# The first feed-forward layers of a sigmoid-attention and gated feed-forward kernel: plain products over 512 tokens against one level of Strassen's algorithm over pairs of batches

## The chip, the cores and the metric

The kernel runs on one core of one Trainium2 chip. A core has a matrix engine (TensorE, PE in the profile, with its weight loads apart as PEld), three engines for element-wise work (VectorE or DVE, ScalarE or ACT, GpSimd or POOL), a queue engine (SyncE or SP) that issues nearly all DMAs here, and 16 DMA engines between DRAM and the on-chip memory SBUF. TensorE writes to PSUM, which DVE and ACT can read and POOL can't. The metric is the device time of one execution in microseconds (us), lower is better.

## The reference

Two stages follow each other: attention with a sigmoid in place of the softmax, and a gated feed-forward layer.

```
def _attn_ref(q, k, v):                       # q, k, v: (8, 12, 448, 64)
    S = q.shape[2]
    scores = q @ k.transpose(0, 1, 3, 2) / sqrt(64) - log(S)
    attn = 1 / (1 + exp(-scores))
    return attn @ v

def _moe_ref(x, w_gate, w_val, w_out):        # x: (3584, 768); w: (768, 1536), (768, 1536), (1536, 768)
    gate = 1 / (1 + exp(-(x @ w_gate)))
    val = x @ w_val
    return gate * val @ w_out
```

x is the attention's output, 8 batches of 448 tokens, with the 12 heads of 64 side by side as 768 columns. The weights come as 64-bit floats, the rest as 32-bit floats. In the kernel each operand of the feed-forward layers is split into a part `hi`, rounded to the type fp32r, and a rest `lo`, and a product is three matmuls: lo x hi, hi x lo, hi x hi.

## The kernel before

Everything is kept transposed: a tile has 128 features as its partitions and tokens along its row. The order on each engine is that in which the code is written (`manual_schedule`); engines meet at semaphores only. One queue, SP, carries the loads and stores in order, and a DMA at its head that has to wait holds up those behind it.

**Attention.** 24 pairs of two heads' pairs (m), each in 7 beats (g). A beat is four score products (L218), one sigmoid over 128x896 on ACT (L221), and the value products of two beats earlier (L235). At the end of a head pair ACT copies one PSUM tile (L245), DVE adds the other (L252), and the result goes to DRAM as x (`store_x`, L189). Beside this run the steps of a generator that turns 64-bit weight words into `hi` and `lo`: a chunk of 128x384 takes eight DVE instructions (L99 to L102, L112 to L114, L118) and one cast on POOL (L141). In this stage it converts the weights of the first 7 of 12 blocks j of 128 hidden features (`convert_tiles`), and they stay in SBUF.

**Feed-forward.** Tokens are taken 512 at a time, 7 tiles t. Part one goes over the 7 tiles with the first 7 blocks, part two with the last 5 (`late`), whose weights are converted during part one, stored to DRAM and fetched back at its end. For each block, `ff_in` computes gate and value (18 matmuls each, L321), then the sigmoid on ACT (L324), the product on DVE (L325), and the split into hh on ACT and hl on DVE (L328, L329). `ff_out` then sums over the blocks for each of 6 output tiles (L339). Part one stores these sums as `part` (L344, L345), part two loads them back and adds them (L362). At the change of a token tile x is split again: xh on ACT (L180), xl on DVE (L181). PSUM has four buffers (`mm`) for all of it.

## Time and profile before

| | |
|---|---|
| median of 3 runs | 1293.74 us (1293.4 to 1294.04) |
| the profiled execution | 1293.55 us, of which the span of its instructions is 1291.5 us |
| granted TensorE clock over the span | 1.0 |
| TensorE matmuls | 7240, busy 1285.3 us |
| DVE, ACT, POOL busy | 464.5, 358.7, 37.5 us |
| DMA | 152.14 MB, mean 118 GB/s |

In the rows of the profile `out<-in 128x512 f32 xN | busy, mean ns | idle` stands for N instructions of one line and shape, their summed time, the mean of one, and the time for which their engine stood idle just before them, with what ended it. Matmuls overlap in the pipeline, so the distance from one start to the next, and not the mean duration, is what a matmul costs. In a timeline the first two numbers are start and duration in us.

### The profile page before, as it was taken

The page shows a single profiled execution, that of the slowest core. Times are in us where ns is not written, and L with a number is a line of the kernel's source. Part 1 is how long each engine was busy: PE and PEld are TensorE (multiplying, and loading weights), DVE is VectorE, ACT ScalarE, POOL GpSimd, SP SyncE. Part 2 cuts the span into 40 slices and gives each one's busy share as a digit, 9 for nine tenths or more (in the row PEclk, how much of TensorE's full clock was granted, in tenths as well). Part 3 has the DMA queues.
Part 4 walks back from the last instruction along what each step waited for, and adds up shares of the span by engine and source line. Part 5 has one row for each costly group of instructions (what it writes and reads, how often), then busy time and mean ns, then how long its engine had stood idle before and what let it go on. Part 6 is the DMA issues. An engine that isn't in the chain of part 4 may idle for free.

```text
span 1291.5 us, 17704 instructions
## 1 busy us (share of the span) xinstructions
PE 1285.3 (100%) x7240; PEld 1003.8 (78%) x7240; DVE 464.5 (36%) x921; ACT 358.7 (28%) x505; POOL 37.5 (3%) x52
## 2 busy tenths in 40 slices
PE   9999999999999999999999999999999999999998
PEld 4445666688888888888888888888888888888887
DVE  6778777345154252461310111202231313131311
ACT  6777777712112112121121121212020201111110
POOL 1112111000000000000000000000000000000000
PEclk9999999999999999999999999999999999999999
DMA  8788777343332332422002015241404131222202
GB/s 299 244 261 279 244 235 234 132 146 96 111 98 86 116 94 77 142 95 102 25 25 74 1 46 201 104 174 54 147 8 139 33 114 49 98 66 82 74 25 81
DMA packets 70928, 152.14 MB, mean 118 GB/s; under 512 B 9408, under 2 KB 26688, under 8 KB 70848
## 3 DMA queue, kind: packets, MB, share of 16 engines
q1 hardware_dynamic: 70704, 150.90, 34.8%
q8 instruction: 56, 0.92, 0.3%
q14 instruction: 24, 0.20, 0.0%
q10 hardware_dynamic: 144, 0.13, 0.0%
HBM read 106.17 MB, written 44.83 MB: 117 GB/s over the span
## 4 chain that ended last, share of the span: by engine, by line
PE 99%; ACT 0%; DVE 0%; DVEq 0%; issue 0%
PE acc L321 53%; PE acc L339 27%; PE av L235 10%; PE sc L218 10%; PE sc L272 0%; ACT a L221 0%; DVE zeros L67 0%; DVE ob L362 0%; DVEq L423 0%; DVE bias L65 0%
## 5 line engine op out<-in xcount | busy, mean ns | idle before, releaser
L321 PE MATMUL acc<-xh,gv 128*128 128x512 f32 x2016 | 623.0, 389 | 0.0
L321 PEld LDWEIGHTS acc<-xh,gv 128*128 128x128 f32 x2016 | 378.5, 188 | 79.2 <-issue 0.7
L321 PE MATMUL acc<-xl,gv 128*128 128x512 f32 x1008 | 392.1, 389 | 0.0
L339 PE MATMUL acc<-hh,wo 128*128 128x512 f32 x1008 | 312.6, 389 | 0.0
L325 DVE TENSOR_TENSOR g<-acc,g 128x512 f32<-128x512 f32 x84 | 58.1, 692 | 598.4 <-PE acc L321 598.4
L339 PEld LDWEIGHTS acc<-hh,wo 128*128 128x128 f32 x1008 | 189.3, 188 | 39.3
L321 PEld LDWEIGHTS acc<-xl,gv 128*128 128x128 f32 x1008 | 189.3, 188 | 39.1
L218 PE MATMUL sc<-qk 64*64 64x448 f32 x1344 | 204.5, 537 | 0.4 <-ACT a L221 0.4
L235 PE MATMUL av<-a,v 64*64 64x448 f32 x1344 | 204.5, 536 | 0.0
L339 PE MATMUL acc<-hl,wo 128*128 128x512 f32 x504 | 196.1, 389 | 0.0
L221 ACT ACTIVATE a<-sc,bias 128x896 f32<-128x896 f32 x168 | 169.3, 1009 | 66.3 <-PE sc L218 62.9
L328 ACT CAST hh<-g 128x512 fp32r<-128x512 f32 x84 | 52.1, 621 | 355.2 <-DVE g L325 355.2
L324 ACT ACTIVATE g<-acc 128x512 f32<-128x512 f32 x84 | 50.3, 599 | 338.2 <-PE acc L321 338.2
L218 PEld LDWEIGHTS sc<-qk 64*64 64x64 f32 x1344 | 80.0, 133 | 52.1 <-issue 24.0
L235 PEld LDWEIGHTS av<-a,v 64*64 64x64 f32 x1344 | 80.5, 133 | 51.2 <-issue 28.1
L339 PEld LDWEIGHTS acc<-hl,wo 128*128 128x128 f32 x504 | 94.6, 188 | 19.6
L329 DVE TENSOR_TENSOR hl<-g,hh 128x512 fp32r<-128x512 f32 x84 | 58.2, 693 | 57.7 <-ACT hh L328 57.7
L344 ACT COPY ob<-acc 128x512 f32<-128x512 f32 x42 | 24.7, 588 | 147.8 <-PE acc L339 147.8
L362 DVE TENSOR_TENSOR ob<-acc,pb 128x512 f32<-128x512 f32 (+1 forms) x43 | 29.0, 677 | 82.5 <-PE acc L339 79.4
L252 DVE TENSOR_TENSOR x<-av,x 128x448 f32<-128x448 f32 x48 | 29.9, 624 | 63.0 <-ACT x L245 57.0
L181 DVE TENSOR_TENSOR xl<-xr,xh 128x512 fp32r<-128x512 f32 x84 | 52.4, 689 | 0.0
L180 ACT CAST xh<-xr 128x512 fp32r<-128x512 f32 x78 | 41.9, 616 | 0.0
(23 smaller groups left out, 331.4 us busy)
## 6 DMA issues: line engine op xcount, KB each, us to landing
xr<-xd SPq DMA_DIRECT2D x84, 256.0 KB, 4.4
qk<-qk SPq DMA_DIRECT2D x23, 896.0 KB, 5.0
v<-vv SPq DMA_DIRECT2D x24, 448.0 KB, 4.5
part<-ob SPq DMA_DIRECT2D x42, 256.0 KB, 2.0
pb<-part SPq DMA_DIRECT2D x42, 256.0 KB, 3.0
y<-ob SPq DMA_DIRECT2D x41, 256.0 KB, 2.0
wraw<-wg SPq DMA_DIRECT2D x24, 384.0 KB, 4.0
wraw<-wv SPq DMA_DIRECT2D x24, 384.0 KB, 3.8
```

The source lines that it names most:

```text
L180: cast(xh[c], xr[c])
L181: nc.vector.tensor_tensor(out=xl[c], in0=xr[c], in1=xh[c], op=ALU.subtract)
L218: nc.tensor.matmul(sc[halves[u], h, :S], lhsT=qkt[halves[h], p, k0:k0 + HP], rhs=qkt[halves[h], p, :S], start=True, stop=True)
L221: nc.scalar.activation(a, sc[:, :, :S], AF.Sigmoid, bias=bias, scale=scale)
L235: nc.tensor.matmul(avs[key][halves[h], :S], lhsT=vt[halves[u], g, h], rhs=a[halves[u], h], start=start, stop=g == last)
L252: nc.vector.tensor_tensor(out=x, in0=other, in1=x, op=ALU.add)
L321: nc.tensor.matmul(acc, lhsT=a, rhs=m, start=n == 0, stop=n == len(terms) - 1)
L324: nc.scalar.activation(g, acc, AF.Sigmoid)
L325: nc.vector.tensor_tensor(out=g, in0=acc, in1=g, op=ALU.mult)
L328: nc.scalar.copy(hh, g)
L329: nc.vector.tensor_tensor(out=hl, in0=g, in1=hh, op=ALU.subtract)
L339: nc.tensor.matmul(acc, lhsT=a, rhs=m, start=n == 0, stop=n == len(terms) - 1)
```

## The change

The first feed-forward layers (gate and value) are computed by Strassen's scheme with seven products in place of eight. A product matrix is cut in two by two: two blocks of hidden features (a pair `jp`) by two halves of the 768 input features on the weights' side, the same two halves by two batches of 448 tokens (a pair `pr`) on x's side. For each pair jp and each of gate and value there are 7 weight operands (four blocks or combinations of them, of which three blocks are used as they are), for each pair of batches 7 combinations of x, and 7 products of 9 matmuls each (`product`), which `unit` puts together: p1 and p5 are copied out of PSUM by ACT, five sums of a PSUM tile and an SBUF tile are made by DVE and two (u4, c22) by POOL.

- The tiles of the feed-forward layers are 448 tokens wide in place of 512. There are two sets of three pairs jp, and each set visits the four pairs of batches: 8 visits of 6 units and 36 output tiles (`out_tile`, 6 matmuls each). The sums over the pairs jp of a set are kept in SBUF (`sums`): the first is copied by ACT or, in the second set, added to `part` by DVE, the others are added by DVE.
- No weights stay in SBUF. Each operand (hi and lo, 384 KB) goes to DRAM after its conversion and is read for each visit through a ring of 7 buffers (`load_operand`), the output weights (256 KB) through a ring of 8 (`load_out`). The load for the ring's next place is issued after the product that frees it.
- The conversion (`convert`) makes the sums of weights too: for gate and value, POOL adds hi and lo again after each chunk and makes four combinations, which ACT and DVE split. The first set is converted beside the attention, the second during the visits to the first set, a step now and then by the count in `tick`.
- x's combinations and their split (`split_x`, 21 steps, 12 of them with a subtraction on POOL, all with a cast on ACT and a subtraction on DVE) stand among the last 18 output tiles of a visit, two steps to a tile at first, then one. For the first visit they stand in the attention.
- The gate's product with the value is made by POOL for two of the four results of a unit.
- PSUM holds four buffers for products (`un`) and four for output tiles (`mm`).

```
+    def convert(words, jps):
...
+        for jp in jps:
+            for t in range(2):
+                f = []
+                for n in (0, 4, None, 6):
                     words.first()
                     yield
                     hi, a, e = words.second()
+                    hl = pool.tile([P, 2, CW], F32R, tag="whl", name="whl")
+                    nc.gpsimd.tensor_copy(hl[:, 0], hi)
+                    finish_lo(hl[:, 1], a, e)
+                    f.append(pool.tile([P, CW], F32, tag=f"wf{len(f)}", name="wf", bufs=1))
+                    nc.gpsimd.tensor_tensor(out=f[-1], in0=hl[:, 0], in1=hl[:, 1], op=ALU.add)
+                    if n is not None:
+                        store(hl, jp, t, n)
                     yield
+                a11, a12, a21, a22 = f
+                for n, (to, x, y, op) in enumerate(((a22, a21, a22, ALU.add), (a22, a22, a11, ALU.subtract),
+                                                    (a21, a11, a21, ALU.subtract), (a12, a12, a22, ALU.subtract))):
+                    hl = pool.tile([P, 2, CW], F32R, tag="whl", name="whl")
+                    nc.gpsimd.tensor_tensor(out=to, in0=x, in1=y, op=op)
+                    nc.scalar.copy(hl[:, 0], to)
+                    nc.vector.tensor_tensor(out=hl[:, 1], in0=to, in1=hl[:, 0], op=ALU.subtract)
+                    store(hl, jp, t, (1, 2, 3, 5)[n])
+                    yield
...
+    def split_x():
+        for n in range(N_OPS):
+            for k in range(KC):
+                b11, b12, b21, b22 = (xs[i, k] for i in range(4))
+                if n == 1:
+                    xs[4, k] = xpool.tile([P, S], F32, tag=f"t{k}", name="t")
+                if n in (1, 2, 3, 6):
+                    to, x, y = {1: (4, 1, 0), 2: (4, 3, 4), 3: (1, 3, 1), 6: (4, 2, 4)}[n]
+                    nc.gpsimd.tensor_tensor(out=xs[to, k], in0=xs[x, k], in1=xs[y, k], op=ALU.subtract)
+                x = xs[(0, 4, 4, 1, 2, 3, 4)[n], k]
+                hi = xpool.tile([P, S], F32R, tag=f"bh{n}{k}", name="bh")
+                lo = xpool.tile([P, S], F32R, tag=f"bl{n}{k}", name="bl")
+                nc.scalar.copy(hi, x)
+                nc.vector.tensor_tensor(out=lo, in0=x, in1=hi, op=ALU.subtract)
+                bs[n, k] = hi, lo
                 yield
...
+        def product(n):
+            acc = un.tile([P, 512], F32, tag="un", name="un")[:, :S]
+            a = ring.pop(0)
             terms = []
+            for k in range(KC):
+                hi, lo = bs[n, k]
+                terms += [(a[:, 1, k], hi), (a[:, 0, k], lo), (a[:, 0, k], hi)]
+            for i, (w, m) in enumerate(terms):
+                nc.tensor.matmul(acc, lhsT=w, rhs=m, start=i == 0, stop=i == len(terms) - 1)
+            load_operand()
...
+        def unit(done):
+            p1, p5, u2, u3, u4 = (sb(n) for n in ("p1", "p5", "u2", "u3", "u4"))
+            c22 = sb("c22")
+            nc.scalar.copy(p1, product(0))
+            tick()
+            nc.scalar.copy(p5, product(1))
+            tick()
+            plus(u2, product(2), p1)
+            plus(u4, u2, p5, nc.gpsimd)
+            tick()
+            plus(u3, product(3), u2)
+            plus(c22, u3, p5, nc.gpsimd)
+            tick()
+            c = sb("c", bufs=2)
+            plus(c, product(4), p1)
+            done(0, c)
+            later.append(lambda: done(3, c22))
...
+            plus(c, product(5), u4)
+            done(1, c)
...
+            plus(c, product(6), u3)
+            done(2, c)
+            tick()
...
+        for v_, (s, pr) in enumerate(visits):
+            js = sets[s]
+            nxt = visits[v_ + 1] if v_ + 1 < len(visits) else None
+            unit(gate)
+            h0 = hidden()
+            if nxt:
+                load_x(nxt[1])
...
+            unit(gate)
+            for t, o in tiles:
+                out_tile(s, pr, js[0], h0, t, o)
+            h1 = hidden()
+            unit(gate)
+            for t, o in tiles[:NO]:
+                out_tile(s, pr, js[1], h1, t, o)
+            h2 = hidden()
+            splits = split_x() if nxt else iter(())
+            for t, o in tiles[NO:]:
+                out_tile(s, pr, js[1], h1, t, o)
+                next(splits, None)
+                next(splits, None)
+            for t, o in tiles:
+                out_tile(s, pr, js[2], h2, t, o)
+                next(splits, None)
```

Three places show how the order on the engines differs. On DVE, at a change of token tile in part two of the kernel before (L181 the split of x, L362 the addition of an output tile):

```order
L325 TENSOR_TENSOR g<-acc,g 128x512
L329 TENSOR_TENSOR hl<-g,hh 128x512
L181 TENSOR_TENSOR xl<-xr,xh 128x512 x6
L362 TENSOR_TENSOR ob<-acc,pb 128x512 x6
L325 TENSOR_TENSOR g<-acc,g 128x512
```

On DVE now, where the last value unit of the first visit ends (g, hl) and its last 18 output tiles begin (`sum<-acc` the addition of an output tile, `bl` the split of x, `whl<-wf` the split of a sum of weights):

```order
L373 TENSOR_TENSOR c<-un,u_4325 128x448
L418 TENSOR_TENSOR g_4247<-c,g_4247 128x448
L422 TENSOR_TENSOR hl<-g_4247,hh 128x448
L373 TENSOR_TENSOR sum_3912<-acc,sum_3912 128x448
L197 TENSOR_TENSOR bl<-x,bh 128x448 x2
L373 TENSOR_TENSOR sum_3923<-acc,sum_3923 128x448
L159 TENSOR_TENSOR whl<-wf,whl 128x384
L197 TENSOR_TENSOR bl<-x,bh 128x448
L197 TENSOR_TENSOR bl<-t,bh 128x448
L373 TENSOR_TENSOR sum_3934<-acc,sum_3934 128x448
```

The six splits stood in one piece ahead of six additions, each of which belonged to 15 matmuls; now 21 splits and, in the first set, steps of the conversion stand between additions that belong to 6 matmuls each.

On POOL, the last instructions of the kernel before, all of them in the attention:

```order
L141 CAST wo_1784<-wt 128x384 x2
L141 CAST gv_2167<-wt 128x384 x4
L141 CAST wo_2168<-wt 128x384 x2
L141 CAST gv_2553<-wt 128x384 x4
L141 CAST wo_2554<-wt 128x384 x2
```

On POOL now, at the place of the first visit that is shown above for DVE (`t` and `x` are combinations of x, `wf` of weights):

```order
L418 TENSOR_TENSOR g_4231<-c,g_4231 128x448
L157 TENSOR_TENSOR wf<-wf 128x384 x2
L192 TENSOR_TENSOR t<-x 128x448 x3
L192 TENSOR_TENSOR t<-x,t 128x448 x2
L157 TENSOR_TENSOR wf<-wf 128x384
L192 TENSOR_TENSOR t<-x,t 128x448
L192 TENSOR_TENSOR x<-x 128x448 x3
L157 TENSOR_TENSOR wf<-wf 128x384
L192 TENSOR_TENSOR t<-x,t 128x448 x3
```

POOL had casts in the attention alone and nothing in the feed-forward layers; now it has operations with two inputs through the whole kernel, 12 of them for the split of x in each of seven visits.

On SP, the end of the attention before (xd the stores of x, `wraw` the raw weight words, `xr` the loads of x), each with the semaphores that it waits for:

```order
L189 DMA xd_4_110<-x 128x448 [waits DMAHW4_49,DVE_49]
L189 DMA xd_5_111<-x 128x448 [waits DMAHW5_49,DVE_49]
L92 DMA wraw<-wg 128x384 [waits DMAHW6_49,PE_49]
L92 DMA wraw<-wg 128x384 [waits DMAHW7_49]
L174 DMA xr<-xd_0_76 128x512 [waits DMAHW0_49,Pool_49]
```

And now (A the ring of weight operands for the products):

```order
L266 DMA xd_4_111<-x 128x448 [waits DMAHW2_49,DVE_49]
L266 DMA xd_5_112<-x 128x448 [waits DMAHW3_49,DVE_49]
L102 DMA wraw<-wg 128x384 [waits DMAHW4_49,PE_49]
L102 DMA wraw<-wg 128x384 [waits DMAHW5_49]
L336 DMA A<-ad_0_0_161 128x768 [waits DMAHW6_49,PE_49]
L336 DMA A<-ad_0_1_162 128x768 [waits DMAHW7_49]
```

The first weights of the feed-forward layers lay in SBUF when the attention ended; now their load stands behind the last store of x and two loads of raw words.

304 lines of the change are left out of this document (158 added, 146 removed).

## The prediction

> **What bounds the kernel now.** I read the page's header, the busy times and the chain that ended last first, then the groups by line, the timeline where the attention hands over, and the windows for DMA.
>
> ```profile
> span 1291.5 us, 17704 instructions
> PE 1285.3 (100%) x7240; PEld 1003.8 (78%) x7240; DVE 464.5 (36%) x921; ACT 358.7 (28%) x505; POOL 37.5 (3%) x52
> ...
> PE 99%; ACT 0%; DVE 0%; DVEq 0%; issue 0%
> PE acc L321 53%; PE acc L339 27%; PE av L235 10%; PE sc L218 10%; PE sc L272 0%; ACT a L221 0%; DVE zeros L67 0%; DVE ob L362 0%; DVEq L423 0%; DVE bias L65 0%
> ```
>
> TensorE is the whole chain, and the lines that the change rewrites (L321) or recuts (L339) are 80% of it. No other engine is over 36%. So the change is worth what it saves in TensorE time, less the waits that it makes where there are none. The groups and the ends of the feed-forward stage give the price of a matmul:
>
> ```profile
> L321 PE MATMUL acc<-xh,gv 128*128 128x512 f32 x2016 | 623.0, 389 | 0.0
> L321 PE MATMUL acc<-xl,gv 128*128 128x512 f32 x1008 | 392.1, 389 | 0.0
> L339 PE MATMUL acc<-hh,wo 128*128 128x512 f32 x1008 | 312.6, 389 | 0.0
> L339 PE MATMUL acc<-hl,wo 128*128 128x512 f32 x504 | 196.1, 389 | 0.0
> ```
>
> ```profile
> 258.62 0.19 PEld L321 LDWEIGHTS acc<-xh,gv 128*128 128x128 f32 x1 [0.71 <-issue]
> 258.62 0.50 PE L321 MATMUL acc<-xh,gv 128*128 128x512 f32 x1
> 258.73 0.19 PEld L321 LDWEIGHTS acc<-xl,gv 128*128 128x128 f32 x1
> 258.96 0.39 PE L321 MATMUL acc<-xl,gv 128*128 128x512 f32 x1
> ...
> 1286.69 0.39 PE L339 MATMUL acc<-hh,wo 128*128 128x512 f32 x1
> ...
> 100.00:200.00 100.00, 100.00 (x1068) 66.39 (x1062) 76.78 (x165) 74.87 (x86) 17.16 (x22) 1.00 0.78 252
> ```
>
> The four groups hold 2016 + 1008 + 1008 + 504 = 4536 matmuls, and their starts run from 258.62 to 1286.69 us: 1028.07/4535 = 226.7 ns from one to the next, without a gap. After the last start 4.8 us of span remain; the profiled execution has 2.05 us outside its span and stands 0.2 us below the median of the runs.
>
> **What the products save.** Seven products of 9 matmuls for each of gate and value, 6 pairs of blocks and 4 pairs of batches make 2 x 7 x 9 x 6 x 4 = 3024 matmuls, as many as now (2016 + 1008), but 448 columns wide in place of 512. The output layer has 8 visits x 36 tiles x 6 = 1728 in place of 1512, with the same columns in all. Together 4752 matmuls of 448. No row shows a 128x128 matmul of 448 columns. If all of 226.7 ns goes with the columns, it takes 198.4 ns. If a part is fixed, it takes more. The attention's matmuls have 448 columns on quarters of the array, 1068 of them in 100 us without a gap (the window's row), 93.6 ns each. If two of them always stream side by side, which is an estimate, 448 columns take 187.3 ns and 512 take 214.0; that leaves 12.7 of 226.7 fixed and makes 200.0 ns. I take this. The weight load does not bound it by this trace: the first two loads start 0.11 us apart (258.62, 258.73), and the first matmul, whose record is 0.11 us longer than the others (0.50 against 0.39), waits that long for its weights, far under 200 ns. The stage is then 4751 x 200.0 = 950.2 us, 77.9 us less than 1028.1. Everything below takes from this.
>
> **The handover.** Now the first weights of the stage are in SBUF and TensorE goes on at 258.62. After the change the first load of the ring stands on SP behind the last store of x and two loads of raw words:
>
> ```profile
> 259.19 0.62 DVE L252 TENSOR_TENSOR x<-av,x 128x448 f32<-128x448 f32 x1 [2.06 <-ACT x L245]
> 260.25 0.88 SPq L92 DMA_DIRECT2D wraw<-wg  x2
> ...
> wraw<-wg SPq DMA_DIRECT2D x24, 384.0 KB, 4.0
> L272 PE MATMUL sc<-zeros 64*64 64x448 f32 x16 | 3.3, 963 | 1.4 <-DVE zeros L67 1.4
> L218 PE MATMUL sc<-qk 64*64 64x448 f32 x1344 | 204.5, 537 | 0.4 <-ACT a L221 0.4
> ```
>
> The store waits for the addition that ends at 259.81; the two raw loads are issued until 261.13; an operand is also 384 KB and lands 4.0 us after its issue: 265.2, so TensorE stands for 6.6 us. Whether it then starts cold as at the kernel's start (963 ns for a matmul that takes 537 later, 16 of them, in groups of 4: at most 16 x 0.43/4 = 1.7 us) the trace can't show. I take 7, between 6 and 8. The six operands behind the first are issued 0.44 us apart and are used 9 x 0.2 = 1.8 us apart, so they are in time.
>
> **DVE and POOL, the term that decides.** DVE takes the conversion's chunk, and the additions, at these prices:
>
> ```profile
> 268.56 0.69 DVE L329 TENSOR_TENSOR hl<-g,hh 128x512 fp32r<-128x512 f32 x1 [0.69 <-ACT hh L328]
> 269.17 0.35 DVE L99 TENSOR_SCALAR wa<-wraw 128x384 uint32<-128x384 uint32 x1
> ...
> 270.62 0.55 DVE L112 SCALAR_TENSOR_TENSOR wt<-wraw,wt 128x384 uint32<-128x384 uint32 x1
> 271.09 0.55 DVE L113 SCALAR_TENSOR_TENSOR wa<-wraw,wa 128x384 uint32<-128x384 uint32 x1
> ...
> 271.95 0.56 DVE L118 SCALAR_TENSOR_TENSOR wa<-wa,we 128x384 fp32r<-128x384 uint32 x1
> ...
> L252 DVE TENSOR_TENSOR x<-av,x 128x448 f32<-128x448 f32 x48 | 29.9, 624 | 63.0 <-ACT x L245 57.0
> ```
>
> A chunk is 272.51 - 269.17 = 3.3 us (1.45 for its first half, to 270.62, and 1.85 for the second). Instructions that follow at once start 0.08 us before the end of the one ahead (0.61 for a record of 0.69, 0.47 for 0.55), so the 0.62 us of an addition at 448 columns costs 0.54, and 0.47 at 384. What POOL does beside DVE shows in five rows of the attention and one of the feed-forward stage, where POOL is idle:
>
> ```profile
> L114 DVE TENSOR_SCALAR we<-wt x40: 657/662/666, 20.0 to 236.9; 128x384 uint32<-128x384 uint32 x40
> L114 DVE TENSOR_SCALAR we<-wt x28: 350/352/355, 271.6 to 577.6; 128x384 uint32<-128x384 uint32 x28
> ...
> 106.26 1.09 DVE L181 TENSOR_TENSOR xl<-xr,xh 128x512 fp32r<-128x512 f32 x1
> 107.27 0.76 DVE L99 TENSOR_SCALAR wa<-wraw 128x384 uint32<-128x384 uint32 x1
> ...
> L181 DVE TENSOR_TENSOR xl<-xr,xh x30: 679/684/686, 321.5 to 663.9; 128x512 fp32r<-128x512 f32 x30
> L180 POOL CAST xh<-xr x5: 733/933/1066, 95.6 to 106.8; 128x512 fp32r<-128x512 f32 x5
> ```
>
> L114, which follows each cast of 384 columns, takes 662 ns beside it and 352 without: the cast holds DVE up for 0.31 us. A cast of 512 makes L181 1.09 in place of 0.68 and L99 0.76 in place of 0.35: 0.41 us. The casts themselves stretch to 1066 ns. So DVE's instructions on SBUF alone and POOL's exclude each other and add up; an addition out of PSUM (L252) is in no row beside POOL, and I take it as free. POOL had 48 casts in the attention; the new kernel gives it some 340 operations with two inputs. No row has one. Its hold lies between that of a cast at 448 columns (0.36, between 0.31 and 0.41) and the longest POOL record (1.07). I take two inputs as two casts, 0.72 us, nearest to the casts that do the same per input.
>
> The place where this ends on TensorE is the last 18 output tiles of a visit: 6 x 0.2 = 1.2 us each, 21.6 in all. Four PSUM buffers let TensorE start tile 18 when DVE has finished the addition of tile 14, so the stretch lasts until then plus 1.3 us. Ahead of the first addition DVE finishes the last value unit (sum, product, wait for ACT's cast, split: some 2.7 us after the last product). Up to the 14th addition its queue holds 14 additions and 19 splits, 33 x 0.54 = 17.8 us; in three of the seven visits that have a next one also 1 to 2 chunks and up to 3 splits of weight sums, 5.5 us on the mean. POOL has 12 subtractions there. Three can run earlier; the other nine wait for splits and alternate with DVE, every second one partly beside an addition: 9 x 0.72 - 4.5 x 0.54 = 4.1 us; in the three visits 3 operations on weights more, 1.2 us. So TensorE waits, in each of these three, 2.7 + 17.8 + 5.5 + 4.1 + 1.2 + 1.3 - 21.6 = 11.0 us, and in the other four 2.7 + 17.8 + 4.1 + 1.3 - 21.6 = 4.3: 33 + 17 = 50 us. With 0.36 for POOL it is 31, with 1.07 it is 74. Who waits behind it: the next visit's products have PSUM buffers of their own and x's first splits are done, so what DVE has left over then is hidden under the next unit, where ACT empties the first two products.
>
> The Trainium skill has a price, in GPSIMD Engine Reference, Elementwise — side-by-side cycle accounting: an addition of two tensors of 2048 columns takes 4497 ns on GpSimd, about 2.2 ns a column, which would be an estimated 1.0 us at 448, and its Specifications name VectorE instructions with two SBUF inputs as those that contend for the shared interface, as L181 does above (1.09 against 0.68). By that price the waits come to 69 us and the sum to 1297.
>
> **The attention.**
>
> ```profile
> 0.00:250.00 250.00, 248.20 (x2618) 147.10 (x2622) 177.34 (x389) 184.41 (x210) 37.47 (x52) 1.00 0.75 247
> ...
> 0.00:100.00 100.00, 98.20 (x1024) 46.06 (x1028) 70.58 (x158) 72.09 (x82) 14.90 (x23) 1.00 0.81 271
> ...
> L221 ACT ACTIVATE a<-sc,bias 128x896 f32<-128x896 f32 x168 | 169.3, 1009 | 66.3 <-PE sc L218 62.9
> ...
> L245 ACT COPY x<-av 128x448 f32<-128x448 f32 x48 | 25.2, 524 | 1.1 <-PE av L235 1.1
> ```
>
> Of 250 us, DVE is busy 177 (71%), ACT 184 (74%), DMA 75% at 247 GB/s. Six chunks fewer take 20 us from DVE; 24 splits of weight sums and 15 more of x add 19; POOL's 60 operations with two inputs add at most 60 x 0.72 = 43, a part of it beside additions from PSUM. ACT gets 24 casts of 384 and 21 of 448 columns, some 23 us at L245's 0.52: 83%, and some of them wait for POOL with a sigmoid behind them. A sigmoid of 1.0 us in a beat of 1.5 has about 1.2 us to spare before the next scores want its PSUM buffer. While x is split (49 beats) all this comes near the beat, elsewhere not. DMA: 42 operand stores and the stores of output weights replace six raw chunks' loads, 62 MB become some 82. At 247/0.75 = 330 GB/s that is 249 us: full, if stores in larger pieces go no faster. Between 0 and 20 us of waits; I take 5, since the slack of 1.2 us covers most single delays.
>
> **Nothing elsewhere.** In the feed-forward stage an operand of 384 KB is wanted each 1.8 us (220 GB/s) and is asked for six products, 10.8 us, ahead; landing takes some 4 us, and x's loads (12 x 224 KB, some 8 us at 330 GB/s) come while six operands are in. The first set lasts 4 x 118.8 us and its waits, 512 us, in which 142 MB move: 277 GB/s, over the 271 of the attention's first 100 us at a share of 0.81, under the 335 that this makes at a full share. Copies and casts on ACT, some 40 us of a visit's 119, lie beside matmuls; the last addition and store are as long as now.
>
> **The sum.** 258.6 + 5 (attention) + 7 (handover) + 950.2 + 50 (waits for additions) + 4.8 + 2.05 = 1278 us, 1.2% under the profiled 1293.55.
>
> **The rivals.**
> 1. The waits stay small, since POOL's hold is a cast's (0.36) or its subtractions run ahead: 31 us or less, none in the attention: 258.6 + 6 + 950.2 + 31 + 6.85 = 1253, down to 1222 with no wait at all. The 36% of DVE speak for it, the 18 tiles' own DVE time (17.8 us and 2.7 ahead) against less than 10.
> 2. Slower: POOL's two-input operations hold DVE longer. By the sum above the waits may be 66 us before the gain is gone, which is reached at 0.95 us for an operation; at 1.07, with 15 in the attention and 8 at the handover, the time is 1312. The price in the skill lies on this side. The stretched casts speak for it, the 0.31 to 0.41 of their own hold against it.
> 3. Slower: the ring starves. If DMA moves no more than the attention's mean of 247 GB/s, 142 MB take 575 us, 63 more than the 512, and the time is 1341; it decides from 528 us on, 269 GB/s. The share of 0.75 at that mean speaks against it, SP's order for it: an operand stands behind stores that wait for DVE and POOL.
> 4. The matmul stays at 226.7 ns, bound by its weights: 4752 x 226.7 = 1077, 127 more than I take, and near 1390 in all, since the waits shrink a little. The 0.11 us between the first two loads speaks against it.
>
> **How the numbers follow.** Forecast 0.42, rival 1 0.2, rival 2 0.26, rival 3 0.08, rival 4 0.03, the rest open. The range is from 1243, in the middle of rival 1, to 1312, the end of rival 2, and leaves out the fewest waits and rival 4. The forecast's own range is 1262 to 1293. About 0.2% (2.6 us) is what a measurement can tell from no change; the forecast's upper edge and rival 2's lower one put 0.08 there, so faster 0.58, slower 0.34.
>
> **What would show it.** Right: starts of the product matmuls 200 ns apart; TensorE idle before output tiles with a DVE addition as the releaser, 8 to 14 us at the end of the first three visits and 2 to 7 of the next four; POOL records of two inputs near or over 0.72 us and splits (L197) well over 0.62. Wrong: a distance other than 198 to 200; waits of the products for the ring's loads; a POOL operation under 0.5 or over 0.95 us of hold; waits in the attention over 20 us.

## The result and the profile after

The changed kernel takes 1409.33 us (median of 4 runs, 1407.84 to 1410.82), the kernel before, run again beside it, 1293.85 (4 runs, 1293.40 to 1294.04). The ratio is 1.0893, with a 95% interval from 1.0874 to 1.0912: slower by 8.9%, where 1.2% faster was forecast, and outside the range.

From the page of the changed kernel: busy times, granted clock, the chain that ended last, and two groups of matmuls.

```profile
span 1407.2 us, 20966 instructions
...
PE 1284.3 (91%) x7456; PEld 1019.8 (72%) x7456; DVE 840.2 (60%) x1466; ACT 467.9 (33%) x769; POOL 447.6 (32%) x388
...
PEclk9999999999999999899989999999899999999999
...
PE 51%; DVE 8%; POOL 8%; DMA 8%; issue 6%; ACT 1%; SPq 0%; POOLq 0%; DVEq 0%; ACTq 0%
...
L362 PE MATMUL un<-bh,A 128*128 128x448 f32 x2016 | 580.0, 367 | 10.4 <-DMA A<-ad 7.6
L442 PE MATMUL acc<-hh,wo 128*128 128x448 f32 x1152 | 370.7, 393 | 85.0 <-DVE sum L373 72.8
```

TensorE was 99% of the chain and is now 51%, though it still looks 91% busy: a record is 367 ns long and starts lie some 200 ns apart, so records overlap and say little. The products (L362) stood 10.4 us in all, the output tiles (L442) 85.0, mostly behind VectorE's additions. The stretches of the second visit (with conversion), the fifth (without) and the last (nothing follows it), each cut ahead of its last 18 output tiles:

```profile
core 0: us, PE busy (x) PEld busy (x) DVE busy (x) ACT busy (x) POOL busy (x), PEclk, DMA share, GB/s
...
441.30:541.10 99.80, 98.78 (x488) 91.21 (x487) 65.98 (x123) 25.11 (x49) 34.55 (x31) 1.00 0.87 305
541.10:586.50 45.40, 28.52 (x109) 22.73 (x108) 37.86 (x62) 12.79 (x25) 24.16 (x20) 0.81 0.40 134
873.40:976.50 103.10, 100.36 (x488) 92.43 (x487) 39.71 (x62) 18.07 (x34) 20.46 (x17) 0.98 0.75 244
976.50:1009.40 32.90, 27.49 (x109) 23.26 (x108) 29.45 (x44) 11.63 (x23) 18.56 (x13) 0.84 0.45 140
1279.70:1380.30 100.60, 99.97 (x488) 91.07 (x487) 39.40 (x62) 17.97 (x34) 20.21 (x17) 1.00 0.66 201
1380.30:1403.40 23.10, 22.13 (x109) 20.01 (x107) 13.32 (x23) 1.13 (x2) 1.46 (x1) 1.00 0.42 145
```

The same 108 matmuls take 23.1 us where no split follows, 32.9 with the splits, 45.4 with splits and conversion; VectorE is busy 13.3, 29.5 and 37.9 us there, POOL 1.5, 18.6 and 24.2. The granted clock falls with it (0.84, 0.81). The other 486 matmuls of a visit take close to 100 us in all three.

Against the terms of the forecast, by the starts of the matmuls in the trace:

| term | forecast | measured |
|---|---|---|
| attention, to the first product (258.6 + 5 + 7) | 270.6 | 298.6 (last value product at 290.5, handover 8.1) |
| distance of the feed-forward's matmuls without waits | 200.0 ns, 950.2 us | 203.5 ns on the mean, 967 us |
| waits in the last 18 tiles of the visits | 50 (3 x 11.0, 4 x 4.3) | 102.6 (18.3, 23.6, 17.9; 10.4, 11.0, 9.5, 10.7; 1.2) |
| waits elsewhere in the feed-forward | 0 | 35, of it 30 in the first 12 tiles of the visits |
| tail and outside the span | 6.85 | 5.8 |

Here a wait is what the starts lie apart beyond 201 ns, in distances that pass it by 60 ns or more; so matmuls at half the clock behind a pause (last section) are in it (152 of them 373 ns apart, 26 us).

### The profile page after: what moved, and what is told of

It reads as the page before. It is cut to its first block, busy times and chain, and to the rows that moved or that the text cites. A ratio compares the mean times of both kernels' runs of the same rounds, so it can differ in the third digit from the quotient of the medians.

```text
span 1407.2 us, 20966 instructions
## 1 busy us (share of the span) xinstructions
PE 1284.3 (91%) x7456; PEld 1019.8 (72%) x7456; DVE 840.2 (60%) x1466; ACT 467.9 (33%) x769; POOL 447.6 (32%) x388
## 4 chain that ended last, share of the span: by engine, by line
PE 51%; DVE 8%; POOL 8%; DMA 8%; issue 6%; ACT 1%; SPq 0%; POOLq 0%; DVEq 0%; ACTq 0%
PE un L362 35%; PE acc L442 14%; POOL t L192 3%; DMA pb<-part 3%; DVE sum L373 2%; POOL x L192 2%; DVE bl L197 2%; POOL g L418 2%; DMA A<-ad 2%; DMA x<-xd 1%; DMA ad<-whl 1%; PE av L244 1%; POOL c L373 1%; PE sc L227 1%; DMA qk<-qk 1%
## 5 line engine op out<-in xcount | busy, mean ns | idle before, releaser
L362 PE MATMUL un<-bh,A 128*128 128x448 f32 x2016 | 580.0, 367 | 10.4 <-DMA A<-ad 7.6
L442 PE MATMUL acc<-hh,wo 128*128 128x448 f32 x1152 | 370.7, 393 | 85.0 <-DVE sum L373 72.8
L362 PEld LDWEIGHTS un<-bh,A 128*128 128x128 f32 x2016 | 379.5, 188 | 44.5 <-issue 8.3
L362 PE MATMUL un<-bl,A 128*128 128x448 f32 x1008 | 369.4, 367 | 0.0
L442 PEld LDWEIGHTS acc<-hh,wo 128*128 128x128 f32 x1152 | 233.3, 203 | 129.5 <-DVE sum L373 94.3
L373 POOL TENSOR_TENSOR u<-u,p 128x448 f32<-128x448 f32 x48 | 56.4, 1175 | 536.0 <-DVE u L373 536.0
L442 PE MATMUL acc<-hl,wo 128*128 128x448 f32 x576 | 223.3, 388 | 0.0
L362 PEld LDWEIGHTS un<-bl,A 128*128 128x128 f32 x1008 | 189.7, 188 | 16.0
L227 PE MATMUL sc<-qk 64*64 64x448 f32 x1344 | 161.7, 551 | 17.7 <-ACT a L230 17.4
L421 ACT CAST hh<-g 128x448 fp32r<-128x448 f32 x96 | 52.7, 566 | 260.9 <-DVE g L418 205.0
L373 DVE TENSOR_TENSOR sum<-acc,sum 128x448 f32<-128x448 f32 x192 | 116.6, 616 | 27.1 <-PE acc L442 26.4
L442 PEld LDWEIGHTS acc<-hl,wo 128*128 128x128 f32 x576 | 117.3, 204 | 9.2
L422 DVE TENSOR_TENSOR hl<-g,hh 128x448 fp32r<-128x448 f32 x96 | 65.8, 688 | 62.9 <-ACT hh L421 62.9
L379 ACT COPY p<-un 128x448 f32<-128x448 f32 x48 | 25.4, 530 | 203.6 <-PE un L362 203.6
```

The costliest lines, as they stand in the source:

```text
L227: nc.tensor.matmul(sc[halves[u], h, :S], lhsT=qkt[halves[h], p, k0:k0 + HP], rhs=qkt[halves[h], p, :S], start=True, stop=True)
L362: nc.tensor.matmul(acc, lhsT=w, rhs=m, start=i == 0, stop=i == len(terms) - 1)
L373: engine.tensor_tensor(out=to, in0=x, in1=y, op=ALU.add)
L421: nc.scalar.copy(hh, g)
L422: nc.vector.tensor_tensor(out=hl, in0=g, in1=hh, op=ALU.subtract)
L442: nc.tensor.matmul(acc, lhsT=w, rhs=m, start=n == 0, stop=n == len(terms) - 1)
```

## The experiments

Theory at the start: POOL's operations with two inputs cost VectorE, and through it TensorE, more than assumed. Rivals: the splits' place in in-order queues; VectorE's own work. "Waits" are those defined above. Runs 1 to 9 were made once each, beside a run of the kernel before (1293.7 to 1293.9 us), runs 10 to 16 four to twelve times.

**1. POOL's two-input operations of the feed-forward on VectorE.**

```
-def split_x():                      +def split_x(engine):      # nc.vector in the feed-forward
-plus(u4, u2, p5, nc.gpsimd)         +plus(u4, u2, p5)          # c22 and the gate products likewise
```

> In the feed-forward stage the two-input operations of POOL (the subtractions of x, u4, c22 and two of the gate's products) go to DVE; those of the weight sums and of the attention stay. Theory (a POOL operation of 1.1 us shuts DVE's SBUF instructions out, so it costs more there than its 0.54 us on DVE itself): TensorE's waits in the last 18 output tiles fall from 18 to 24 us to about 14 in the visits with conversion and from 10 to about 6 in the others, and the time from 1409 to about 1370. Rival (DVE's own queue is what is too long, and POOL works beside it): 11 more instructions of 0.54 us ahead of the 14th addition make every such stretch 6 us longer, and the time is about 1450.

1441.58 us: near the rival's number. The last 18 tiles of visits 2 and 5:

```profile
544.40:592.30 47.90, 31.54 (x109) 24.69 (x108) 39.41 (x73) 12.23 (x24) 7.72 (x8) 0.75 0.38 129
992.20:1031.00 38.80, 29.73 (x109) 24.23 (x109) 29.95 (x54) 11.81 (x23) 0.00 (x0) 0.74 0.38 125
```

In visit 5 VectorE is busy as long as with POOL's help (29.95 against 29.45 us), but the stretch is 38.8 us in place of 32.9. The subtraction, the cast and the trailing part now go VectorE, ScalarE, VectorE, and VectorE stands 8.9 us in this stretch, 7.4 of them until a cast is done. That POOL simply costs VectorE more than it takes off it is refuted: ten instructions more and POOL's work beside it come to the same busy time.

**2. No splits for visits 2 to 8; 8. splits without POOL's subtractions; 4. no second conversion.**

```
2: -splits = split_x() if nxt else iter(())    +splits = iter(())
8: -if n in (1, 2, 3, 6):                      +if n in (1, 2, 3, 6) and subtract:     # False from visit 2 on
4: -convert(words, sets[1]), 32 * SET          +iter(()), 0       # set 2 reads set 1's operands
```

> Left out: the combinations and splits of x for the second to the eighth visit (the first visit's are used again; x is still loaded). Theory (the splits between the additions hold up TensorE): the waits in the last 18 output tiles, 103 us in all, go but for a few us, and the time is about 1305. Rival (the additions are late since the loads of the rings and the conversion hold up the queues, whatever stands between them): less than half of it goes, and the time stays over 1355.

> The changed kernel, in which the splits for visits 2 to 8 leave out POOL's 12 subtractions (the 21 casts and 21 VectorE subtractions of the trailing part stay, on the loaded x instead of its combinations). Theory (POOL's subtractions of 1.13 us or more, in order behind the conversion's pair, hold ScalarE's cast, that holds VectorE's trailing part, and that the additions out of PSUM behind it): the waits of the last 18 output tiles, 102 us in seven visits, fall under 30, time about 1335, close to the 1329 without any split. Rival (VectorE's own work per output tile, 0.62 + 1.17 x 0.84 us and the conversion against 1.22 us of matmuls): 60 us or more stay, time 1365 or above.

> Left out: the conversion of the second set of weights (the second set of visits uses the first set's operands, so the loads are as many). Theory (in visits 1 to 4 the conversion's DVE and POOL instructions stand between the additions): the waits in the last 18 output tiles of the first three visits fall from 18 to 24 us to the 10 of the others, and the time is about 1375. Rival (it is its DMA, 35 MB in the first set, that hurts): landing times of the ring's loads fall and waits for them go, but the waits for DVE's additions stay over 15 us in these visits.

1329.28, 1357.97 and 1354.9 us. The last 18 tiles of visits 2 and 5, two rows for each kernel in this order:

```profile
529.50:558.30 28.80, 24.43 (x110) 22.17 (x110) 22.79 (x45) 2.42 (x5) 9.47 (x10) 0.88 0.62 204
924.60:948.10 23.50, 22.55 (x110) 20.24 (x110) 13.35 (x23) 1.13 (x2) 1.46 (x1) 1.00 0.67 213
```

```profile
533.00:569.80 36.80, 27.02 (x110) 21.86 (x109) 33.77 (x63) 12.04 (x26) 9.51 (x9) 0.91 0.46 156
946.70:972.10 25.40, 23.94 (x110) 19.80 (x110) 23.10 (x44) 10.94 (x23) 1.46 (x1) 1.00 0.53 171
```

```profile
527.40:559.90 32.50, 26.55 (x109) 21.86 (x108) 29.30 (x44) 11.64 (x23) 18.54 (x13) 0.89 0.42 135
925.40:957.00 31.60, 24.33 (x110) 19.60 (x109) 28.83 (x44) 11.64 (x23) 18.54 (x13) 1.00 0.42 136
```

Visit 5 reads cleanly. Without splits VectorE has 13.35 us to do and the stretch is 23.5. With casts and trailing parts it has 23.1, and the stretch is 25.4. The 12 subtractions on POOL, which give VectorE nothing to do, raise VectorE's busy time to 29.45 with the same 44 instructions, and the stretch to 32.9: they lengthen the splits beside them (0.63 us for each of the 21 without the subtractions, 0.84 with them). Of the 101 us of waits in these stretches of visits 1 to 7, 51 are left without the subtractions and 24 without any split. So the subtractions make about half, and the rest of the split some 27. The 54 us that run 4 is faster are the conversion's: 27 in this stretch of visits 1 to 3, 15 in the first 12 tiles of visits 3 and 4, 6 before the first product, the rest in smaller pieces. These shares overlap and can't be added: in visits 1 to 3 the waits of 59.7 us fall to 37.0 without the subtractions, to 19.0 without the splits, to 32.9 without the conversion. The theories of runs 2 and 4 hold in the main; theory and rival of run 8 are both half right.

**9. POOL's subtraction two splits ahead.**

```
-sub(n, k); nc.scalar.copy(hi, x)      +sub(*steps[i + 2]); nc.scalar.copy(hi, x)
```

> The changed kernel with one edit: POOL's subtraction of a split is issued two splits before ScalarE's cast that needs it (in the feed-forward and in attention alike the same work; attention keeps its order). Theory A (latency: the wait is that of a cast issued right behind the subtraction it needs): waits of the last 18 output tiles halve in visits 4 to 7, 10.4, 11.0, 9.5, 10.7, to 5 or less, and fall by a third in the visits with conversion; time 1375 to 1390. Theory B (throughput: in 22 us of output tiles POOL has 12 subtractions of 1.3 us and some 5 us of conversion): no visit changes by over 2 us, time within 10 us of 1409.

1407.37 us, and the waits in no visit's last 18 tiles change by over 2 us, as theory B said: the latency of one subtraction is not the cause.

**3 and 5. Attention: two orders of the conversion; feed-forward: splits from the value unit on.**

```
3: +yield                                   # between POOL's sum of weights and ScalarE's cast
   +next(x_loads, None)                     # one load of x a beat in place of 12 at once
5: -nc.scalar.copy(hl[:, 0], to)            +nc.gpsimd.tensor_copy(hl[:, 0], to)   # attention
   +bufs=4  # whl;   +split_x(2)            # POOL two splits ahead, both in the attention
   +h2 = hidden(lambda: next(splits, None)) # one split per product, then one per tile
```

> Two changes of order, meant for the attention: ACT's cast of a weight sum stands one step of the conversion behind POOL's operation, and the 12 loads of x for the first visit are issued one in a beat. Theory (ACT waits in order for POOL, with a sigmoid and then TensorE behind it, and v's load stands behind 12 loads on SP): the attention ends at about 268 us in place of 290, the wait of 5.6 us at 112 us is gone, and the time is about 1385. Rival (in the attention DMA is full at 283 GB/s, and any order gives the same): the attention ends at 285 or later.

> Nothing is left out; the same work stands elsewhere. Two edits, read apart because they lie in different stretches. (a) Feed-forward: the 21 splits of the next x begin one per product in the visit's last value unit and then go one per output tile, instead of 21 in the last 18 output tiles. Theory (too much work per output tile there, on DVE's own queue and on POOL's in front of it): the waits of the last 18 output tiles, 18.3, 23.6, 17.9, 10.4, 11.0, 9.5, 10.7 us in the changed kernel, fall to about half, -40 to -50 us in all, and none appears in the unit. Rival (each split costs PE what POOL's hold adds to VectorE wherever it stands): the waits move into the value unit and the sum stays within 10 us. (b) Attention: the leading part of the weight sums is cast on POOL instead of ScalarE, four staging buffers instead of two, x loaded one tile per beat, POOL's subtractions of x two splits ahead. Theory (ScalarE's sigmoid stands behind casts that wait for POOL or for a store): last matmul of attention at 262 to 272 us instead of 290.5. Rival (POOL's longer use of the port slows VectorE and the beats with it): still 285 or more. Time by the theories about 1345, by the rivals 1405.

1409.94 and 1407.03 us. What ScalarE's in-order queue does to the attention shows in the changed kernel's timeline of ACT; the second fence is ACT's waits in run 3, where the stalls have another place and the last value product is as late (291.0 us):

```profile
24.57 1.01 ACT L230 ACTIVATE a<-sc,bias 128x896 f32<-128x896 f32 x1
28.90 0.51 ACT L158 CAST whl<-wf 128x384 fp32r<-128x384 f32 x1 [3.33 <-POOL wf L157]
29.32 1.90 ACT L230 ACTIVATE a<-sc,bias 128x896 f32<-128x896 f32 x2
```

```profile
ACT bh L202 <- POOL t L198: 19.0, 5, 8.2
ACT whl L159 <- POOL wf L157: 8.2, 3, 3.9
ACT whl L159 <- DMA ad<-whl: 4.6, 3, 2.6
```

A cast that waits 3.33 us for POOL holds two sigmoids, and TensorE behind them. Run 3 brings TensorE's wait for v from 4.7 to 1.2 us and leaves the waits for sigmoids (17.4 us before, 19.9 now). Run 5 takes these casts off ScalarE, and TensorE's waits for sigmoids fall to 0.4 us: the last value product comes at 274.3 us in place of 290.5, 2 us past the end of its theory's range. Three more edits stand in run 5's attention (four staging buffers, spread loads of x, subtractions ahead), and no run separates them from the casts. What TensorE waits for there now is q and k, 7.2 us in 6 waits. In its feed-forward the waits only moved, from the last 12 tiles to the six ahead of them (11 to 15 us a visit): ScalarE's casts now stood behind POOL inside the value unit.

**6, 7, 10, 11, 12. Output tiles over all three pairs of blocks, and then one queue after another.** The visit makes its six units first, then 12 tiles of 18 matmuls whose sums stay in PSUM, so the additions on VectorE fall from 24 (first set) or 36 (second set) a visit to 0 or 12.

```
6:  +for q in range(SET): unit(gate); hs.append(hidden(q, step))
    +for t, o in tiles: out_tile(s, pr, hs, t, o, step)     # 18 matmuls; operands loaded ahead of the handover
7:  splits in the tiles alone, two each; attention: x's subtractions on VectorE, weight sums all on POOL
10: +due.append(lambda: nc.sync.dma_start(out=a_dram...))   # stores one conversion step later
    six of the first set's 36 weight chunks converted in visit 1; first two tiles interleaved
11: -due in the feed-forward; the six chunks back in the attention; stores of tiles one tile later; gate products on VectorE
12: +due again, wa and wt with two buffers; the six chunks in visit 1 again
```

> Nothing is left out. The attention edits of e5, and: the first six weight operands are loaded during the last beats of attention into a buffer of their own; a visit does its three gate and value units first and then 12 output tiles of 18 matmuls that add all three pairs of blocks in PSUM, so that the additions of partial sums on VectorE fall from 24 to 36 a visit to 0 (first set) or 12 (second); splits of the next x one per product of the last value unit, then two per output tile of 3.6 us; the leading part of the weight sums on POOL in the feed-forward too. Theory (the queues per output tile cost the time, the products themselves cost 200 to 207 ns a matmul): waits of the feed-forward under 25 us, handover under 3 us, feed-forward 965 to 990 us, time 1235 to 1265, faster than before. Rival (POOL's share of the port and the conversion slow the rest wherever they stand): waits of 60 us or more, time 1290 or above.

> Nothing is left out. Edits on the merged kernel before it: the splits of the next x stand in the 12 output tiles alone (two per tile of 3.6 us, POOL's subtraction one split ahead), none in the value unit; the 12 loads of x one per product; a part of y's sum is requested before the store of the tile beside it. Attention: the trailing part of the weight sums on POOL too, x's subtractions there on VectorE. Theory (each engine runs its queue in order; in the merged kernel ScalarE's copy out of PSUM and its hh stood behind a cast that waited for POOL's subtraction, 90.6 us of such waits, and PE met it at the first output tile): the first output tile's waits, 9.4 to 15.0 us a visit, fall under 2, the third unit's 5.1 to 7.2 (12 x loads ahead of a weight operand) under 1; feed-forward 1141 -> 980 to 1000; attention's last matmul 260 to 268; time 1240 to 1270, below before. Rival (capacity: VectorE, ScalarE and POOL together cannot do the visit's work beside 128 us of products): waits of 60 us or more come back elsewhere, time 1300 or more.

> Nothing is left out. Edits on the merged kernel with splits in the tiles (1306.6 us): stores of converted weights are issued one conversion step later, so that SP's queue does not stand behind them with the loads of q, k and v (its waits for POOL and VectorE at that line were 79 us; PE's longest wait in attention, 6 us, was for such a load); six of the 36 weight chunks of the first set are converted in the first visit instead of attention (4.7 MB less there, where DMA was 0.82 to 0.94 busy); the value unit that comes last before the tiles takes all its gate products on VectorE, and the first two output tiles add the third pair of blocks last; x loads one per two products. Theory (each remaining stall is a queue that stands behind an engine that is late): attention's last matmul 260 to 268 us instead of 275.3, first output tiles' waits 5 to 7 us a visit to under 2, feed-forward 1024.8 to 985-1000, time 1250 to 1270. Rival (the transfers of attention, 80 MB, and the conversions fill what time there is: capacity): attention 272 or more, waits come back elsewhere, time 1290 or more.

> Nothing is left out. Edits on the run before: conversion of the first set all in attention again; in the feed-forward the converted weights are stored at once (VectorE had waited 44.2 us there for buffers whose stores came a step later) and the trailing part of a weight sum is taken one step after POOL's part; stores of output tiles are issued one tile later and behind the loads of output weights (SP had stood 112.5 us behind the store of a tile whose copy ScalarE had not made, and PE 24.9 us behind output weights); the gate products all on VectorE; no conversion step in the last three products before the tiles. Theory (each of the five waits is a queue behind a late engine): attention's last matmul 263 to 268 us; feed-forward visits with conversion 125 to 129 us (146 at most before), without 122 to 124; time 1255 to 1275, below before by 1.5 to 3%. Rival (the conversion's and the splits' work on VectorE and POOL is too much for a visit, whatever the order): visits with conversion 131 or more as in the 1306.6 us kernel, time 1290 or more.

> Nothing is left out. Edits on the run before (1292.6 us; visits without conversion 121.0 us, with it 127 to 140; attention's last matmul 275.8): in the feed-forward too every converted weight is stored one conversion step later, now with two buffers for the words on VectorE, and the trailing part of a weight sum is taken by POOL; six output weights ahead instead of seven; again six weight chunks of the first set converted in the first visit and not in attention. Theory (SP's queue stood 131.6 us behind stores of converted weights that VectorE had not made, and the loads of operands and output weights behind them were what PE waited for, 28.7 us in 8 waits, and at half clock after): visits with conversion 122 to 126 us, attention 262 to 266, time 1245 to 1262, below before by 2.5 to 4%. Rival (the conversion's own work on VectorE and POOL): visits with conversion stay at 130 or more, time 1275 to 1292.

1418.81, 1306.64, 1334.06, 1292.56 and 1290.95 us; the ratio to before is 1.031 (1.0293 to 1.0327) for run 10, 0.9991 (0.9977 to 1.0005) for 11, 0.9969 (0.9958 to 0.998) for 12. Of the waits, the rows that name the queue in runs 6, 7 (SP), 10 (SP, DVE, PE) and 11 (SP):

```profile
ACT bh L210 <- POOL t L199: 90.6, 29, 7.7
...
PEld acc L468 <- ACT hh L447: 71.8, 12, 12.1
```

```profile
SPq L137 <- DVE whl L130: 40.8, 10, 6.8
SPq L137 <- POOL whl L161: 38.4, 18, 4.0
```

```profile
DVE wa L111 <- DMA od<-wa: 44.2, 11, 6.4
...
PE acc L485 <- DMA wo<-od: 24.9, 17, 6.5
```

```profile
SPq L503 <- ACT pb L502: 112.5, 38, 12.0
```

```profile
SPq L142 <- DVE whl L130: 88.2, 18, 9.7
...
SPq L142 <- DVE whl L190: 43.4, 17, 5.4
```

Run 6 has 192 additions fewer on VectorE and is slower than the change: the splits in the value unit put ScalarE's hh behind casts that wait for POOL. Run 7 takes them out, spreads the loads of x and puts POOL's subtractions one split ahead: 112 us less. Run 10 mends the attention (last value product 263.3 us, 275.3 in run 7) and loses in the feed-forward, where VectorE then waits for the late stores. Runs 11 and 12 mend that: visits without conversion now take 121 to 123 us, close to what 594 matmuls take (121 at 203.5 ns), those with it 127 to 140 and 132.5 to 135.6. The attention shows what mended it in run 10. Run 11 keeps its late stores and takes the six chunks back: 275.8 us, as in run 7. Run 12 has both: 264.3. So the six chunks make the 12 us, and the late stores alone none, though the theories of runs 10 and 11 named SP's order. TensorE's waits for q and k go with them (10.8 us in run 11, 3.9 in run 12); here in runs 7 and 10:

```profile
PE sc L251 <- DMA qk<-qk: 12.6, 7, 6.0
```

```profile
PE sc L268 <- DMA qk<-qk: 3.3, 2, 2.2
```

None of the five reached its theory's time; each time lies where its rival put it.

**13 and 14. The conversion's transfers in another queue.**

```
-nc.sync.dma_start(raw, ...), (a_dram, ...), (o_dram, ...)     +nc.gpsimd.dma_start   (13)
                                                               +nc.scalar.dma_start   (14)
```

> Nothing is left out. The run before (1290.95 us) with one edit: in the feed-forward the raw weight words are loaded and the converted ones stored from POOL's queue instead of SP's. Theory (SP's queue order): with SP left to operands, output weights, x and tiles, the visits with conversion fall from 132.5, 133.6, 132.8, 135.6 us to 122 to 127, and the time to 1250 to 1270. Rival (the conversion's own work on VectorE and POOL): they stay at 130 or more, time 1283 or more; if POOL is held longer by issuing transfers, above 1291.

> Nothing is left out. As the run beside it, but the conversion's transfers go into ScalarE's queue, where the store of converted weights can wait for VectorE with the copies out of PSUM behind it. Theory (queue order): SP's share of the gain comes, but ScalarE's copies now stand behind stores; visits with conversion between 124 and 132 us, time 1255 to 1285. Rival (the conversion's own work): 130 or more, time 1283 or more.

1308.11 us (ratio 1.0124, 1.0085 to 1.0162) and **1283.16 us (0.9927, 0.9906 to 0.9948)**: run 14 is 0.7% faster than the kernel before, the fastest here. Its visits 1, 2, 5 and 8:

```profile
264.80:388.40 123.60, 121.23 (x597) 111.48 (x595) 85.25 (x151) 32.25 (x61) 44.72 (x41) 1.00 0.84 286
388.40:521.70 133.30, 122.95 (x595) 112.74 (x594) 101.38 (x172) 36.07 (x70) 61.44 (x57) 0.96 0.85 287
792.30:913.30 121.00, 120.81 (x595) 111.42 (x594) 56.20 (x86) 30.38 (x58) 29.93 (x24) 1.00 0.78 245
1155.50:1275.90 120.40, 120.40 (x595) 111.33 (x593) 40.17 (x66) 19.42 (x36) 13.84 (x12) 1.00 0.65 198
```

The first visit, with conversion, takes 123.6 us (132.5 in run 12), so the conversion's own work fits in a visit that takes over no unfinished splits. Visits 2 to 4 gain nothing by the new queue (133.3 to 135.9 us): they lose 11 to 13 us in their first unit, where ScalarE's copy of the first product stands behind the last splits. In run 13 the first units of these visits lose 13 to 17 us, and POOL is busy 66 us more than in run 12 (508.6 against 442.8). The Trainium skill (Trainium Kernel Development and Optimization, Key Constraints) says that issuing DMAs from several engines saves only issue time, since all run on the same 16 DMA engines; here the move to ScalarE's queue, the one edit of run 14, took 8 us off the time (the first visit gains 9), and the move to POOL's cost 17.

**15 and 16. Splits first, conversion after; conversion kept out of the last three tiles.**

```
15: four splits per tile, then 6 ticks in each of the last seven tiles
16: four splits per tile, 4 ticks in tiles 5 to 9; the rest of the conversion in the units
```

> Nothing is left out. The 1283.2 us kernel with one edit: in the 12 output tiles the splits come first (four per tile, done by the sixth) with no conversion beside them, and the conversion steps follow in the last seven tiles (two or three per tile). Theory (a conversion pair between two splits in the three queues makes a round of 9 us for three splits, so the splits run into the next visit, whose first copies ScalarE makes 10 us late): the waits of 11.8, 11.2, 12.6 us in the first unit of visits 2 to 4 fall under 3, visits with conversion 122 to 126 us, time 1250 to 1260. Rival (the conversion's own work fills VectorE and POOL): the waits move to the end of the tiles or to the units, visits stay at 130 or more, time 1275 or more.

> Nothing is left out. The 1283.2 us kernel with one edit: in the output tiles the splits come first, four per tile; conversion steps stand in tiles 5 to 9 alone (about two per tile) and in the units (one per two products), none in the last three tiles. Theory (order in the queues alone): the first unit's waits of visits 2 to 4 (11.8, 11.2, 12.6 us, and 13.2, 10.6, 15.6 in the run before this) fall under 3, visits with conversion 121 to 126 us, time 1245 to 1262. Rival (the conversion's own work): more conversion in the units, where VectorE already has some 33 us of other work in 76, brings waits there; visits stay at 130 or more, time 1275 or more.

1292.83 us (0.9993, 0.9982 to 1.0003) and 1292.94 (0.9995, 0.9983 to 1.0007). What TensorE waited for in the feed-forward, in run 15 (with one of ScalarE's waits behind it) and in run 16:

```profile
PE un L409 <- ACT p L425: 31.6, 3, 13.6
...
ACT p L425 <- POOL whl L191: 11.3, 1, 11.3
```

```profile
PE un L409 <- DVE c L420: 13.5, 10, 3.1
PE acc L498 <- ACT hh L473: 9.2, 4, 4.1
PE un L409 <- DMA A<-ad: 7.0, 2, 4.4
```

With splits first, the first units of visits 2 to 4 wait as long as before (13.2, 10.6, 15.6 us): ScalarE's copies now stand behind stores of converted weights that POOL or VectorE has yet to make. In run 16 these waits fall to 2.9, 3.2 and 6.1, and some 10 us a visit come back in the later units and the tiles, in visit 1 too (12 us, 3 in run 14): behind VectorE's sums (13.5 us), ScalarE's hh (9.2) and loads of operands (7.0). Each order moved the waits to another queue or left them. Whether an order without them exists is open: visit 1 of run 15 took 121.9 us, its visits 2 to 4 136 to 140.

## Why the prediction was wrong, step by step

The time is 131 us over the sum of 1278: 53 in the last 18 tiles, 35 in waits elsewhere, 28 in the attention with the handover, 17 in the distance of the matmuls, 1 less at the end. No single step makes the miss. Three failed: POOL's price and the terms beside it in the last 18 tiles, the slack of the attention, and "nothing elsewhere"; the matmul's price was mis-sized.

- **What the products save: right in kind, 17 us short.** Starts lie 199 to 207 ns apart, 203.5 on the mean, against 200.0 and outside the 198 to 200 that the prediction allowed. The fourth rival (226.7) is refuted. If a matmul costs a fixed part and a part by the column, 226.7 at 512 and 203.5 at 448 columns make the fixed part 41 ns, an estimate, where the prediction took 12.7 from the attention's matmuls: as far as that reading holds, the step that mis-sized it is that two of those always stream side by side.
- **The handover: right** (8.1 us for 7), and gone in run 6, where the first operands are loaded ahead (0.5 us from the last value product to the first product).
- **The last 18 tiles: place and mechanism right, the terms too small.** "I take two inputs as two casts, 0.72 us". All rows of POOL's two-input operations at 448 columns lie above the upper bound of 1.07:

```profile
L192 POOL TENSOR_TENSOR t<-x,t x48: 1126/1492/1548, 143.4 to 1268.6; 128x448 f32<-128x448 f32 x48
...
L373 POOL TENSOR_TENSOR u<-u,p x48: 1143/1154/1347, 306.8 to 1374.1; 128x448 f32<-128x448 f32 x48
...
L373 DVE TENSOR_TENSOR sum<-acc,sum x192: 606/615/625, 385.1 to 1403.6; 128x448 f32<-128x448 f32 x192
```

  The fastest takes 1126 ns, beside VectorE's splits the median is 1492. The Trainium skill's price (GPSIMD Engine Reference, Elementwise — side-by-side cycle accounting; 1.0 us at 448 by the prediction's estimate) was nearer than the rows of casts. With 1.13 the prediction's own formula gives 11.0 + 12 x 0.41 = 15.9 and 4.3 + 9 x 0.41 = 8.0 us, with 1.49 it gives 20.2 and 11.2: measured are 17.9 to 23.6 and 9.5 to 11.0. That the records fit so well is in part luck, for run 8 gives the terms one by one. In visits 4 to 7 POOL's subtractions are worth 7.1 us of wait on the mean, where the formula had 4.1, and 3.3 to 3.5 are left without them, where it had 0.2. By the formula (9 x hold - 4.5 x 0.54 = 7.1) the hold is 1.05 us, less than any record. In visits 1 to 3 the conversion is worth 6 to 13 us (run 4), where the formula had 6.7. That additions out of PSUM go free beside POOL was right too (606 to 625 ns with a POOL at 32%).
- **The second rival came true in its sign.** POOL's hold, 1.05 us by run 8, is past the 0.95 that the prediction named and just under the 1.07 at which it ended the range; that the time lies 97 us past this end comes from the other terms. A bound drawn from one cast's longest record was no bound for the records of an operation with two inputs (1.13 at the least).
- **The attention: 5 us taken, 32 measured.** The failed step is "the slack of 1.2 us covers most single delays". A delay is that of an in-order queue: 3.33 us for a cast behind POOL, and 4.65 us for a load of v that SP issued behind twelve loads of x (9.18 us):

```profile
100.74 9.18 SPq L180 DMA_DIRECT2D x<-xd  x12
```

  TensorE stood 17.4 us for sigmoids and 4.7 for v; the rest goes with the clock behind these waits (granted 0.95 to 0.98 in the attention, 1.00 before). Run 5, with the casts on POOL, has 16 of the 32 us back. Another 11 to 12 come back only when six chunks leave the attention (runs 10 and 12 against 7 and 11), and with them waits for loads of q and k. The prediction had this term too, DMA "full" by 82 MB, and priced it with the slack.
- **"Nothing elsewhere": 35 us.** The step "copies and casts on ACT lie beside matmuls" failed in the first 12 tiles of visits 3 and 4 (5.3 and 9.4 us). The waits of visit 4 in this place:

```profile
ACT whl L158 <- DMA ad<-whl: 9.0, 1, 9.0
PEld acc L442 <- ACT sum L449: 7.6, 1, 7.6
```

  A cast of a weight sum waited for the store of the one before, and the copies out of PSUM behind it. Without the second conversion (run 4) both visits have no such wait. In visits 5 to 7 some 4 us each are left, where VectorE's additions wait for the first set's sums to come back (61.8 us in 30 waits of the second set, most of them hidden).
- **The third rival, a starved ring, was wrong:** products waited 7.6 us for operands, all of it at the handover. The mean of 242 GB/s says little, since TensorE stood for other reasons; run 14's first visit moves 286 GB/s, past the 269 at which this rival would decide, and takes 123.6 us.

## What to carry to other kernels

An algorithm that trades matmuls for element-wise work pays by the stretch: here 108 matmuls (22 us) had 29 to 38 us of VectorE's time to cover, while the same engine was idle 34 to 63 us in the rest of the visit. Before building, lay the new work over the stretch in which its buffers allow it, price it by a run without it where that can be had (POOL's records, 1.13 us at the least, were not its hold, 1.05, and a cast's were further off), and draw each in-order queue (ScalarE's, POOL's and SP's too): a cast or a store that waits for another engine is a wait of everything behind it. Where the tiles can be cut so that the additions stay in PSUM, and the queues are set in order, as in run 14, the seven products do win, 0.7% in place of the 6% that their matmuls alone suggest.

## What the runs showed of the hardware that was not expected

- **Two paces.** Where nothing is waited for, the changed kernel's feed-forward matmuls keep one of two paces. In the first, five distances repeat: three of 202 or 203 ns, one of 199 or 200, one of 206 or 207, 202.7 on the mean (some 3330 of the 4751 distances). In the second all are 206 or 207, 206.7 on the mean (some 1080). A pace nearly always holds until the next wait: the last visit starts with 242 distances of the second and goes on, behind a wait, in the first. Run 14 has the first nearly throughout (4530 distances against 136), run 2 half and half. What sets the pace was not tried.
- **Half the clock behind a wait.** The wait for v and what follows it, in the changed kernel's attention:

```profile
110.07 0.93 PE L227 MATMUL sc<-qk 64*64 64x448 f32 x8
115.65 1.77 PE L244 MATMUL av<-a,v 64*64 64x448 f32 x8 [4.65 <-DMA v<-vv]
117.20 1.72 PE L227 MATMUL sc<-qk 64*64 64x448 f32 x8
118.69 1.72 PE L244 MATMUL av<-a,v 64*64 64x448 f32 x8
120.19 1.42 PE L227 MATMUL sc<-qk 64*64 64x448 f32 x8
121.44 0.92 PE L244 MATMUL av<-a,v 64*64 64x448 f32 x8
```

  Groups of 8 take 1.5 us for some 5 us, and 0.75 after that; the granted clock from 115.6 to 120.5 us is 0.50. In the feed-forward of the changed kernel and of runs 6, 11, 14 and 16 all 24 waits over 4 us are followed so (6 to 14 matmuls 373 ns apart), which adds 2 to 3 us to most of them: a wait of 5 us costs 7 to 8. The Trainium skill gives an idle window of some 3.4 us for this (TensorE: Matmul & The Clock Gate, Part 1). The traces differ from it and show the same behind shorter waits: of the waits with no other among the 40 matmuls ahead, 11 of the 16 from 1.8 to 2.9 us are followed by 7 or 8 matmuls 373 ns apart, and none of those from 0.8 to 1.8 us.
